# Where the flags that pick the 32nd largest score are computed: one VectorE instruction for two items, or two GpSimd compares

## The chip, the cores and the metric

The kernel runs on one core of a Trainium2 chip. The metric is the device time of one execution in microseconds (us); a run's time is compared as a median over several executions. The engines are TensorE (PE; its weight loads are PEld), VectorE (DVE), ScalarE (ACT), GpSimd (POOL) and SyncE (SP, which here only issues DMAs). Each engine takes its instructions in the order in which the program lists them; between engines, and between dependent instructions of one engine, semaphores make an instruction wait.

## The reference

Attention with top-k selection for 8 batches of 8 heads, 576 queries and keys of 64 dimensions, and then a highway layer over the 512 joined columns:

```python
scores = scale * q @ k.T                       # 576 x 576 for each batch and head
kth = the 32nd largest score of each row
attn = softmax(scores where scores >= kth, else -1e9)
x = attn @ v                                   # heads side by side: 4608 x 512
H = max(x @ w_h, 0);  T = sigmoid(x @ w_t + b_t)
out = T * H + (1 - T) * x
```

What matters here is `kth`: one number for each of the 36864 rows of scores.

## The kernel before

**Units, items and steps.** 128 rows of scores (576 columns) of one head, or two half-filled heads for the rows that are left over, make a unit, called an item here. Two items make a pair. There are 288 items and 144 pairs, and the loop `step(i)` handles pair i in one pass, together with the pairs next to it: scores for pair i+2 on PE, the search for candidates of pair i+1 on DVE, the threshold of pair i, the masking of pair i-1, and the product with V of pair i-3. The last pair is handled in `finish`, the first candidates in `begin`. The order on each engine is written out by hand: the calls in `step` are the program order (`tc.manual_schedule`).

**How the 32nd largest is found.** DVE takes the 8 largest of each sixth of a row (`segments`, L353, 12 instructions a pair). `refine` (L366 to L382) merges these 48 candidates: `high` and `low` are the larger and the smaller of two sorted lists, `neg` is `high` negated, four further 8-largest instructions (L373, L376) and two more (L378, L382) give for each item a lower threshold, `wall[THR]`, about the 24th largest. ACT then counts how many of the 576 scores lie above that threshold (`mask_count`, L397: a sign with an accumulated sum, `csum`), and PE adds a mask to the scores in PSUM (`mask_add`, L410), so that DVE can take the 8 largest below the threshold (`below`, L420). The threshold and these 8 are nine candidates for the 32nd largest. Which of them it is follows from the count: `pidx` holds the nine counts that are possible, and the flags `hit` are one where `csum` equals the entry of `pidx`. The flags are multiplied with the nine candidates (`pick_a`, L436, on POOL) and summed (`pick_b`, L439, on DVE). That sum is `kth`.

**The order around the change in `step(i)`.**

- DVE: 12 of L353 for pair i+1, two L420 for pair i, `high` (L366), `low` (L368), the flags (L426), `neg` (L370), two L373, two L376, `pick_b` (L439), L378, then the masking of pair i-1: L450, L382, L460 (or L465).
- POOL: the biases of the pair (`biases`, L391, which wait for the masking L460 of the step before), a compare of 576 columns with `kth` (`above_one`, L454), one piece of "pool work" of the highway layer (L564, L610, L611 or L624: 512 columns, some 256), the product (`pick_a`, L436), and in most steps the issue of a DMA (L187, L182, L582 or L694).
- ACT: counts, exponentials, copies of scores from PSUM and copies for the highway layer.

In `finish` the flags are made by the same function, and the product with the candidates is DVE's (L996).

Of the kernel before, what the change touches and what calls it, by code (L numbers as in the profile page):

```python
# [10 lines left out]
ALU = mybir.AluOpType  # L11
# [15 lines left out]
def kernel(  # L27
# [10 lines left out]
    nc = tc.nc  # L38
    P = nc.NUM_PARTITIONS
# [54 lines left out]
    NPK = TOP_K - RANK + 1  # L94
    pidx = consts.tile([P, NPK], FP32)
# [15 lines left out]
    csum = consts.tile([P, NU], FP32)  # L111
    nc.vector.memset(wall[:, 0:2, KTH : KTH + 1], 0.0)

    def kth(u):
        return wall[:, u + 2, KTH : KTH + 1]
# [158 lines left out]
    def spare(n):  # L274
        if "t" not in po:
            po.update(t=pso_tile(), n=0)
        for _ in range(n):
            nc.tensor.matmul(  # L278
                po["t"][:, 4 * DE : BANK],
                ident_b[:],  # L280
                cst[:, 0 : BANK - 4 * DE],
                start=True,
                stop=True,
                skip_group_check=True,
            )
# [121 lines left out]
    def mask_add(ps, m1, s):  # L407
        cuts = ((0, MAIN), (MAIN, S)) if s == 0 else ((0, rem), (rem, S))
        for s0, s1 in cuts:
            nc.tensor.matmul(  # L410
                ps[:, s0:s1], ident_b[:], m1[:, s0:s1], start=False, stop=True, skip_group_check=True
            )
# [7 lines left out]
        nc.vector.max(wall[:, u, THR + 1 : KTH], ps)  # L420


    def hits(pair):
        u0, u1 = pair[0], pair[1] + 1
        hit = cpool.tile([P, 2, NPK], FP32, name="hit")
        nc.vector.tensor_tensor(  # L426
            hit[:],
            pidx[:].unsqueeze(1).to_broadcast([P, 2, NPK]),
            csum[:, u0:u1].unsqueeze(2).to_broadcast([P, 2, NPK]),
            ALU.is_equal,  # L430
        )
        return hit

    def pick_a(pair, hit):
# [6 lines left out]
    def above(u, sc):  # L441
        r = epool.tile([P, S], BF16, name="r")
        nc.scalar.activation(r[:], sc, AF.Relu, bias=eb(u), scale=BIGK)  # L443
        return r
# [17 lines left out]
    def keep(u, sc, e):  # L462
        ep = eps_sb[u % NEP]
        pad = (u % 2) * (SP - S)
        return ep, nc.vector.scalar_tensor_tensor(  # L465
            out=ep[:, pad : pad + S],
            in0=sc,
            scalar=kth(u),
            in1=e[:],
            op0=ALU.is_ge,  # L470
            op1=ALU.mult,
        )
# [6 lines left out]
    def transposes(ep):  # L479
        et = etpool.tile([P, nck, P], BF16, name="et")  # L480
        nc.sync.dma_start_transpose(et[:], ep[:])
        return et
# [4 lines left out]
    def values(pair, ets, vb, pso, col):  # L487
        for s, u in enumerate(pair):
            b, qt, heads = units[u]
            r0, ql = row_of(pair), rem if qt == nfull else P  # L490
            for gi, h in enumerate(heads):
                for c in range(nck):
                    vc = (c - s) % nck
                    nc.tensor.matmul(  # L494
                        pso[r0 : r0 + ql, col : col + DE],
                        ets[s][:, c, gi * P2 : gi * P2 + ql],
                        vb[:, h, vc, :],
                        start=(c == 0),
                        stop=(c == nck - 1),
                    )  # L500
                col += DE
        return col

    def pso_tile():
        return ops.tile([P, BANK], FP32, tag="po", name="pso")

    def xs_copy(h0, n, pso, xs, r0=0, r1=P):
        nc.scalar.copy(xs[r0:r1, h0 * DE : h0 * DE + n], pso[r0:r1, 0:n])  # L508
# [145 lines left out]
    def blk_xt(k, ps):  # L654
        ng = shape_of(k["qt"])[1]
        k["xT"] = fpool.tile([P, n_g, P], BF16, name="xT")
        for g in range(ng):
            nc.tensor.transpose(ps[:, g * P : (g + 1) * P], k["x"][:, g * P : (g + 1) * P], ident_f[:])
        nc.scalar.copy(k["xT"][:, 0:ng, :], ps[:, 0 : ng * P].rearrange("p (g j) -> p g j", j=P))
# [32 lines left out]
    def do_add(i):  # L692
        dst, src, then = adds.pop(0)
        nc.gpsimd.dma_start(dst, src, accum_op=ALU.add)  # L694
        stores.append((i + 2, then))
# [247 lines left out]
    def finish():  # L943
        i = NG - 1
        pr, pu = pairs[i], pairs[i - 1]
        cur, old = st[i], st[i - 1]

        def values_of(g, n):
            return values(pairs[g], st[g]["et"], vbs[(B - 1) % 2], po["t"], n)

        def xs_of(qt, h0, n):
            if (B - 1, qt) not in xs_t:
                xs_t[B - 1, qt] = xpool.tile([P, H * DE], FP32, name="xs")
            xs_copy(h0, n, po["t"], xs_t[B - 1, qt])
            po["t"] = pso_tile()
            return dict(b=B - 1, qt=qt, xs=xs_t[B - 1, qt])

        def masked(unit, s, of):
            return keep(unit[s], of["sc"][s], of["e"][s])

        def bank(tile, k):
            return tile[:, k * BANK : (k + 1) * BANK]


        z = blocks[-1]
        values_of(i - 3, 0)
        mask_add(cur["ps"][0], cur["m"][0], 0)
        spare(6)
        while late:
            late.pop(0)()  # L970
        if "xT" not in z:
            blk_xt(z, fps.tile([P, 512], FP32, tag="fp", name="fp"))
        while adds:
            do_add(i)
        relu = above(pu[0], old["sc"][0])
        zh = fps.tile([P, 512], FP32, tag="fp", name="fp")
        ep, last = masked(pu, 1, old)
        old["et"][1] = transposes(ep)
        if pool_work:
            after(do_work(nc.gpsimd, dm), last)  # L980
        below(pr[0], cur["ps"][0])
        mask_add(cur["ps"][1], cur["m"][1], 1)
        project(zh, z["qt"], z["xT"], wh, False)
        below(pr[1], cur["ps"][1])
        es = [expo(u, cur["sc"][s]) for s, u in enumerate(pr)]
        cur["e"] = es
        x1 = xps.tile([P, 3 * BANK], FP32, tag="x", name="xs")
        project(bank(x1, 1), z["qt"], z["xT"], wt, True)
        blk_gate(z, bank(x1, 1))
        n = values_of(i - 2, 2 * DE)  # L990
        ya = xs_of(nfull - 1, H // 2, n)

        hit = hits(pr)
        ep, _ = keep_min(pu[0], old["e"][0], relu)
        old["et"][0] = transposes(ep)
        nc.vector.tensor_tensor(hit[:], hit[:], wall[:, pr[0] : pr[1] + 1, THR:KTH], ALU.mult)  # L996
        pick_b(pr, hit)
        x2 = xps.tile([P, 3 * BANK], FP32, tag="x", name="xs")
        cur["et"] = [etpool.tile([P, nck, P], BF16, name="et") for s in range(2)]
        turned = None  # L1000
        for s, home in enumerate((bank(x2, 1), bank(x1, 0))):
            ep, last = masked(pr, s, cur)
            turned = home.bitcast(BF16)[:, 0:SP]
            for c in range(nck):
                nc.tensor.transpose(turned[:, c * P : (c + 1) * P], ep[:, c * P : (c + 1) * P], ident_b[:])
            nc.scalar.copy(cur["et"][s][:].rearrange("p c q -> p (c q)"), turned)
        sure(0, wall[:, 2 : NU + 2, KTH], 1.0)
        sure(1, wall[:, 0:NU, TOP], -1.0)
        values_of(i - 1, 0)
        blk_norm(ya)  # L1010
        blk_xt(ya, bank(x1, 2))
        n = values_of(i, 0)
        yb = xs_of(nfull, 0, n)
        project(bank(x1, 0), ya["qt"], ya["xT"], wh, False)
        do_work(nc.vector, NG * dm)
        nc.vector.scalar_tensor_tensor(cond[:], wall[:, 0:NU, THR + 1], ABOVE, wall[:, 0:NU, THR], ALU.mult, ALU.add)
        while stores:
            stores.pop(0)[1]()
        sure(2, cond[:], 1.0)
        blk_norm(yb)  # L1020
        blk_xt(yb, bank(x2, 2))
        project(bank(x1, 1), ya["qt"], ya["xT"], wt, True)
        blk_gate(ya, bank(x1, 1))
        blk_diff(z, zh)
        store(*blk_out(z))
        project(bank(x2, 0), yb["qt"], yb["xT"], wh, False)
        bg = fps.tile([P, 512], FP32, tag="fp", name="fp")
        project(bg, yb["qt"], yb["xT"], wt, True)
        for j in range(3):
            nc.tensor.matmul(po["t"][0:1, 0:1], cnt[:, j : j + 1], ones[:], start=(j == 0), stop=(j == 2))  # L1030
        blk_diff(ya, bank(x1, 0))
        store(*blk_out(ya))
        blk_gate(yb, bg)
        nc.vector.tensor_scalar(flag[:], po["t"][0:1, 0:1], 3.0 * P * NU - 0.5, None, ALU.is_ge)
        blk_diff(yb, bank(x2, 0))
        return blk_out(yb)
# [102 lines left out]
```

## Time and profile before

| | |
|---|---|
| median of 3 runs | 806.49 us (806.15 to 808.53) |
| the profiled execution | 806.17 us |
| its span, first to last instruction | 804.5 us |
| granted TensorE clock | 0.996 |
| VectorE busy | 772.8 us, 96% of the span |
| ScalarE busy | 757.2 us, 94% |
| TensorE matmuls busy | 686.7 us, 85% |
| GpSimd busy | 559.9 us, 70% |

"Busy" is the time in which at least one of an engine's instructions is under way. A row of a group ends with the busy time of the group, the mean of one instruction in ns, and behind the bar the idle time of the engine just before these instructions and what ended it. A row of a timeline gives start, duration, engine, line, operation, what is written and read, the count, and in brackets idle time with what ended it. Instructions of one engine overlap: the next one starts while the last one still writes.

### The profile page before, as it was taken

What the parts mean: (1) busy time and instruction counts of PE and PEld (TensorE: products, weight loads), DVE (VectorE), ACT (ScalarE), POOL (GpSimd) and SP (SyncE); (2) the same over time, 40 slices, a digit from 0 to 9 for tenths busy, and PEclk for the clock granted to TensorE, in tenths of its full rate; (3) what the DMA queues carried; (4) which work ended last, traced back from release to release, by engine and by line L of the source; (5) the groups of instructions that cost most, each with busy time, mean ns of one, the idle gap of its engine ahead of it and who ended that gap; (6) DMA issues with size and microseconds to landing.
All of it is one profiled execution on the core that took longest, in us unless ns stands there. A gap on an engine that the chain in (4) does not pass through costs nothing.

```text
span 804.5 us, 20583 instructions
## 1 busy us (share of the span) xinstructions
PE 686.7 (85%) x6369; PEld 494.7 (61%) x6459; DVE 772.8 (96%) x4020; ACT 757.2 (94%) x1401; POOL 559.9 (70%) x712
## 2 busy tenths in 40 slices
PE   7889998888888888888987889888888888988884
PEld 5666766566666666566665666666666566665662
DVE  5999999999999999999999999999999999999996
ACT  5999999999999999999999999999999999999984
POOL 2666867777777767777767776777776777766750
PEclk9999999999999999999999999999999999999998
DMA  6789968996799667998669766898767996555653
GB/s 121 87 137 159 134 116 140 141 143 93 140 152 148 108 96 137 154 131 125 102 135 159 125 113 107 150 156 126 112 121 136 160 124 109 90 106 110 108 90 88
DMA packets 346359, 100.37 MB, mean 125 GB/s; under 512 B 330624, under 2 KB 338432, under 8 KB 346240
## 3 DMA queue, kind: packets, MB, share of 16 engines
q1 hardware_dynamic: 291024, 79.16, 54.1%
q0 software_dynamic: 53536, 19.34, 22.6%
q8 instruction: 53, 0.87, 0.4%
q10 hardware_dynamic: 1680, 0.46, 0.3%
q14 instruction: 66, 0.54, 0.2%
HBM read 31.72 MB, written 9.44 MB: 51 GB/s over the span
## 4 chain that ended last, share of the span: by engine, by line
ACT 37%; DVE 32%; PE 23%; DMA 4%; issue 3%; SPq 1%; another core or an unknown queue 0%; DVEq 0%; ACTq 0%
ACT m L397 15%; DVE wall L420 12%; DVE cand L353 9%; ACT e L416 7%; ACT sc L348 6%; PE pso L278 5%; ACT r L443 4%; PE xs L309 4%; PE xs L326 3%; DVE ep L450 3%; DMA xT<-xb 3%; PE fp L522 3%; PE xs L410 3%; PE pso L494 2%; ACT xs L508 2%
## 5 line engine op out<-in xcount | busy, mean ns | idle before, releaser
L353 DVE MAX8 cand<-xs 128x8 f32<-128x96 f32 x1728 | 297.5, 248 | 11.4 <-PE xs L335 6.2
L278 PE MATMUL pso<-cst,ident_b 128*128 128x252 bf16 x1841 | 246.8, 272 | 42.8 <-ACT xs L508 40.4
L454 POOL TENSOR_SCALAR ro<-sc,wall 128x576 bf16<-128x576 f32 x135 | 232.8, 1724 | 0.0
L416 ACT ACTIVATE e<-sc,be 128x576 bf16<-128x576 f32 x288 | 226.5, 787 | 0.1
L278 PEld LDWEIGHTS <-ident_b 128*128 128x128 bf16 x1841 | 173.4, 98 | 81.4 <-issue 49.5
L420 DVE MAX8 wall<-xs 128x8 f32<-128x576 f32 x288 | 204.3, 751 | 5.6 <-PE xs L410 3.5
L309 PE MATMUL xs<-kT,qT 64*128 64x256 f32 x1024 | 145.3, 400 | 30.6 <-DVE high L366 26.2
L348 ACT COPY sc<-xs 128x1152 f32<-128x1152 f32 x144 | 161.0, 1118 | 0.7 <-DVE cand L353 0.6
L309 PEld LDWEIGHTS xs<-kT,qT 64*128 64x128 f32 x1024 | 93.0, 186 | 61.3 <-issue 37.6
L397 ACT ACTIVATE m<-xs,wall 128x576 int8<-128x576 f32 x144 | 107.4, 746 | 18.2 <-DVE wall L382 17.1
L436 POOL TENSOR_TENSOR hit<-hit,wall 128x18 f32<-128x18 f32 x143 | 32.4, 227 | 121.2 <-DVE hit L426 114.0
L397 ACT ACTIVATE m<-sc,wall 128x576 int8<-128x576 f32 x144 | 111.4, 773 | 0.0
L443 ACT ACTIVATE r<-sc,be 128x576 bf16<-128x576 f32 x143 | 109.9, 769 | 0.0
L410 PE MATMUL xs<-m,ident_b 128*128 128x512 bf16 (+1 forms) x512 | 92.7, 274 | 17.3 <-ACT m L397 15.2
L494 PEld LDWEIGHTS <-et 128*128 128x128 bf16 (+1 forms) x1600 | 68.6, 100 | 19.2 <-issue 3.5
L391 POOL TENSOR_TENSOR be<-wall,fac 128x4 f32<-128x4 f32 x144 | 29.2, 203 | 72.5 <-DVE ep L460 53.7
L410 PEld LDWEIGHTS <-ident_b 128*128 128x128 bf16 x576 | 51.7, 97 | 44.8 <-issue 24.1
L494 PE MATMUL pso<-vb,et 128*128 128x65 bf16 (+1 forms) x1600 | 74.4, 194 | 4.2 <-DMA et<-ep 0.3
L450 DVE TENSOR_TENSOR ep<-e,r 128x576 bf16<-128x576 bf16 x143 | 64.6, 452 | 0.2 <-ACT r L443 0.2
L318 PEld LDWEIGHTS xs<-kd,qT 128*128 128x128 f32 x256 | 38.1, 188 | 42.5 <-issue 42.1
L318 PE MATMUL xs<-kd,qT 128*128 128x128 f32 x256 | 62.5, 326 | 0.0
L460 DVE TENSOR_TENSOR ep<-e,ro 128x576 bf16<-128x576 bf16 x135 | 60.7, 449 | 0.0
(127 smaller groups left out, 1028.9 us busy)
## 6 DMA issues: line engine op xcount, KB each, us to landing
kin<-in_k_dram SPq DMA_DIRECT2D x64, 128.0 KB, 2.9
qin<-in_q_dram SPq DMA_DIRECT2D x62, 128.0 KB, 3.1
out_dram<-s SPq DMA_DIRECT2D x30, 256.0 KB, 2.8
s<-h POOLq DMA_DIRECT2D x29, 256.0 KB, 4.0
et<-ep SPq DMA_TRANSPOSE x286, 3.3
xb<-x POOLq DMA_DIRECT2D x30, 128.0 KB, 3.0
vb<-in_v_dram POOLq DMA_DIRECT2D x28, 128.0 KB, 4.8
vb<-in_v_dram POOLq DMA_DIRECT2D x24, 64.0 KB, 3.1
```

Of the source, the lines that this page charges most:

```text
L278: nc.tensor.matmul(po["t"][:, 4 * DE : BANK], ident_b[:], cst[:, 0 : BANK - 4 * DE], start=True, stop=True, skip_group_check=True,)
L309: nc.tensor.matmul(ps[:, mo + n0 : mo + n0 + 256], qT[r : r + D, hp, qs : qs + P], kT[r : r + D, hp, n0 : n0 + 256], start=(n0 == 0), stop ...
L318: nc.tensor.matmul(ends, qT[:, hp, qs : qs + P], kd[:, hp, :], start=True, stop=True)
L348: nc.scalar.copy(sc[:], both)
L353: nc.vector.max(cand[:, s, :], sc[:, s * SEG : (s + 1) * SEG])
L397: nc.scalar.activation(m1[:].bitcast(I8)[:, 1 : 2 * S : 2], ps, AF.Sign, bias=wall[:, u, THR : THR + 1], scale=ABOVE, accum_out=csum[:, u ...
L410: nc.tensor.matmul(ps[:, s0:s1], ident_b[:], m1[:, s0:s1], start=False, stop=True, skip_group_check=True)
L416: nc.scalar.activation(e[:], sc, AF.Exp, bias=tb(u), scale=scale)
L420: nc.vector.max(wall[:, u, THR + 1 : KTH], ps)
L443: nc.scalar.activation(r[:], sc, AF.Relu, bias=eb(u), scale=BIGK)
L454: nc.gpsimd.tensor_scalar(r[:], sc, kth(u), None, ALU.is_ge)
L494: nc.tensor.matmul(pso[r0 : r0 + ql, col : col + DE], ets[s][:, c, gi * P2 : gi * P2 + ql], vb[:, h, vc, :], start=(c == 0), stop=(c == nc ...
```

## The change

The flags are no longer made by one DVE instruction for both items, which reads `pidx` and `csum` as two broadcast tensors (18 columns), but by two compares on GpSimd, one for each item: nine columns of `pidx` against one number per row, that item's column of `csum`. The product that follows stays on GpSimd, now directly behind the two compares. In the last step (`finish`) the flags stay on VectorE, as two compares. All other instructions keep their places: DVE has 143 instructions less, and on POOL the two compares stand right ahead of the product in each of 143 steps. (`in1=e` for `in1=e[:]` names the same tile.)

```diff
-    def hits(pair):
+    def hits(pair, eng=nc.gpsimd):
         u0, u1 = pair[0], pair[1] + 1
         hit = cpool.tile([P, 2, NPK], FP32, name="hit")
-        nc.vector.tensor_tensor(
-            hit[:],
-            pidx[:].unsqueeze(1).to_broadcast([P, 2, NPK]),
-            csum[:, u0:u1].unsqueeze(2).to_broadcast([P, 2, NPK]),
-            ALU.is_equal,
-        )
+        for s in range(2):
+            eng.tensor_scalar(hit[:, s, :], pidx[:], csum[:, u0 + s : u0 + s + 1], None, ALU.is_equal)
         return hit
...
-            in1=e[:],
+            in1=e,
...
-        hit = hits(pr)
+        hit = hits(pr, nc.vector)
```

## The prediction

> **What bounds the kernel now.** I read the page's first lines, then the busy time of the stretch in which all steps of the loop lie (17.5 to 785 us), then the groups, then one step in order of time. The profiled execution took 806.17 us, of which 804.5 are the span, so 1.67 us lie around it; the median of the three runs is 806.49 us. The sum is made against 806.17.
>
> ```profile
> span 804.5 us, 20583 instructions
> PE 686.7 (85%) x6369; PEld 494.7 (61%) x6459; DVE 772.8 (96%) x4020; ACT 757.2 (94%) x1401; POOL 559.9 (70%) x712
> ACT 37%; DVE 32%; PE 23%; DMA 4%; issue 3%; SPq 1%; another core or an unknown queue 0%; DVEq 0%; ACTq 0%
> core 0: us, PE busy (x) PEld busy (x) DVE busy (x) ACT busy (x) POOL busy (x), PEclk, DMA share, GB/s
> 17.50:785.00 767.50, 665.16 (x6182) 479.98 (x6270) 751.28 (x3923) 740.42 (x1369) 557.33 (x699) 1.00 0.79 126
> ```
>
> In the loop DVE is busy for 751.28 of 767.50 us: 16.2 us idle over 143 steps. ACT has 27.1 us idle. Both bind, in turns. GpSimd (POOL) has 210 us idle, so by totals the move looks free. But what counts is the moment at which GpSimd works, and that shows only in one step in order of time (DVE and POOL rows, and one of ACT).
>
> ```profile
> 261.26 0.19 ACT L397 ACTIVATION_READ_ACCUMULATOR m<-sc,wall 128x1 f32 x1
> 262.10 1.41 DVE L420 MAX8 wall<-xs 128x8 f32<-128x576 f32 x2
> 262.16 1.26 POOL L624 TENSOR_TENSOR h<-h,tt 128x512 f32<-128x512 f32 x1
> 263.43 0.19 DVE L366 TENSOR_TENSOR high<-cand 128x48 f32<-128x48 f32 x1
> 263.53 0.20 DVE L368 TENSOR_TENSOR low<-cand 128x48 f32<-128x48 f32 x1
> 263.65 0.17 DVE L426 TENSOR_TENSOR hit<-pidx,csum 128x18 f32<-128x18 f32 x1
> 263.74 0.18 DVE L370 TENSOR_SCALAR neg<-high 128x48 f32<-128x48 f32 x1
> 263.83 0.26 DVE L373 MAX8 en<-low 128x8 f32<-128x24 f32 x2
> 263.90 0.23 POOL L436 TENSOR_TENSOR hit<-hit,wall 128x18 f32<-128x18 f32 x1 [0.48 <-DVE hit L426]
> 264.18 0.15 DVE L439 TENSOR_REDUCE wall<-hit 128x2 f32<-128x18 f32 x1
> ```
>
> See here: POOL ends its pool work at 263.42, sits idle for 0.48 us, and starts the product (L436) 0.08 us after the flags (L426) end on DVE. In just that idle stretch DVE runs `high`, `low` and the flags, each of which reads two tensors of SBUF. The product starts 0.47 us after `high`.
>
> **What is removed.** 143 instructions L426 of 0.17 us. They overlap their neighbours, so one takes from its start to that of `neg`: 263.74 - 263.65 = 0.09 us. Not all of that comes back. `neg` reads `high` and the first L373 reads `low`, so the flags now fill time in which these are still being written. The trace has one refinement without flags, ahead of the loop:
>
> ```profile
> 12.49 0.21 DVE L366 TENSOR_TENSOR high<-cand 128x48 f32<-128x48 f32 x1
> 12.62 0.20 DVE L368 TENSOR_TENSOR low<-cand 128x48 f32<-128x48 f32 x1
> 12.73 0.18 DVE L370 TENSOR_SCALAR neg<-high 128x48 f32<-128x48 f32 x1
> 12.85 0.27 DVE L373 MAX8 en<-low 128x8 f32<-128x24 f32 x2
> ```
>
> From `high` to L373 it is 0.36 us there and 0.40 with flags; from `low`, 0.23 against 0.30. I take 0.05 us a step: 143 x 0.05 = 7.2 us off DVE (bounds: 143 x 0.04 = 5.7 and 143 x 0.09 = 12.9). In the last step the flags stay on DVE as two compares; the second is hidden by the wait for ReLU that follows there, and I cost it at nothing (0.1 us without that cover).
>
> **What is added.** Two compares of 9 columns a step on POOL, ahead of the product. The trace has no such small compare there. Nearest rows:
>
> ```profile
> L454 POOL TENSOR_SCALAR ro<-sc,wall 128x576 bf16<-128x576 f32 x135 | 232.8, 1724 | 0.0
> L436 POOL TENSOR_TENSOR hit<-hit,wall 128x18 f32<-128x18 f32 x143 | 32.4, 227 | 121.2 <-DVE hit L426 114.0 <-DVE neg L370 6.5 <-DMA et<-ep 0.7
> L391 POOL TENSOR_TENSOR be<-wall,fac 128x4 f32<-128x4 f32 x144 | 29.2, 203 | 72.5 <-DVE ep L460 53.7 <-DVE wall L382 10.8 <-DVE ep L465 5.3
> ```
>
> One compare lies between 0.20 (4 columns) and 1.72 us (same operation, 576 columns). I take 0.22, by the 18- and 4-column rows; two started 0.03 us into one another (as L454 starts behind L391) hold POOL for about 0.41 us. They wait for ACT's counts, which were there at 261.45, two microseconds before POOL was free: this wait costs nothing. Queued behind them on POOL are the product, one DMA issue, and the biases (L391). The product now waits for the second compare and for L420, no longer for the flags; with POOL free early it could start at about 263.59 instead of 263.90.
>
> **What is moved onto the path: a hold on DVE.** In a few steps of before, POOL was still busy when `high` came up:
>
> ```profile
> L366 DVE TENSOR_TENSOR high<-cand x144: 183/190/655, 12.5 to 780.3; 128x48 f32<-128x48 f32 x144
> 283.76 1.27 POOL L610 TENSOR_TENSOR s<-h,x 128x512 f32<-128x512 f32 x1 [0.81 <-ACT h L609]
> 284.44 0.66 DVE L366 TENSOR_TENSOR high<-cand 128x48 f32<-128x48 f32 x1
> 285.01 0.20 DVE L368 TENSOR_TENSOR low<-cand 128x48 f32<-128x48 f32 x1
> ```
>
> `high` has a median of 0.19 us, but here it lasted 0.66, until POOL's sum was done (285.03), and `low` started 0.57 us after it where 0.10 is usual: DVE lost 0.47 of the 0.59 us that POOL still had. So a hold costs the rest of POOL's work less 0.12 us. The compares fill just the gap that kept this rare. `high` comes up 0.47 us before the product's present start, so it is held in each step where POOL's idle time before the product is below 0.47 + 0.41 - 0.12 = 0.76 us. These are 75 of 143 rows; the first and the last:
>
> ```profile
> 81.61 0.23 POOL L436 TENSOR_TENSOR hit<-hit,wall 128x18 f32<-128x18 f32 x1 [0.36 <-DVE hit L426]
> 769.16 0.23 POOL L436 TENSOR_TENSOR hit<-hit,wall 128x18 f32<-128x18 f32 x1 [0.50 <-DVE hit L426]
> ```
>
> Their mean idle time is 0.54 us, so `high` comes 0.22 us later in each: 75 x 0.22 = 16.5 us. If POOL lets DVE in between the two compares, the second compare and the product come late for L439 instead, which has only 0.05 us in hand (263.90 + 0.23 against 264.18); I cost both cases alike.
>
> By the Trainium skill ("SBUF — State Buffer", section "Who interferes with whom"), a VectorE instruction with two SBUF inputs and a GpSimd one that reads SBUF exclude each other for the whole instruction, and the later one blocks fully. By that rule the 0.12 us fall away; 90 rows would count instead of 75, and the hold would come to 26.5 us in place of 16.5. The trace's 0.47 of 0.59 us speaks for a little less, and I keep it.
>
> **The product's new place.** `neg` has one input; whether POOL holds that kind too shows in another tensor-scalar of DVE:
>
> ```profile
> L557 DVE TENSOR_SCALAR rinv<-xs x38: 157/162/483, 50.2 to 770.1; 128x8 f32<-128x8 f32 x31, 128x4 f32<-128x4 f32 x7
> 147.04 0.99 POOL L187 DMA_DIRECT2D vb<-in_v_dram  x1 [0.29 <-issue]
> 147.51 0.48 DVE L557 TENSOR_SCALAR rinv<-xs 128x8 f32<-128x8 f32 x1
> ```
>
> It lasted 0.48 instead of 0.16 us, to the end of POOL's issue. So the product, when it starts up to 0.31 us earlier, can run beside `neg` (due at about 263.67, product until 263.82) and hold it by 0.15 us, or 0.03 after the 0.12 are taken off. I take 0.05 us a step: 143 x 0.05 = 7.2 us (bounds 0 and 143 x 0.15 = 21).
>
> **The sum.** DVE's stream: -7.2 + 16.5 + 7.2 = +16.5 us. How much of it reaches the end? The chain of work that ended last has 50 pieces of L426 among 143 steps, first and last
>
> ```profile
> 28.44 0.09 DVE hit L426
> 763.86 0.09 DVE hit L426
> ```
>
> so a small change on DVE counts for 35%; in the other steps ACT or PE binds. A longer DVE binds in more steps, at most in all. I take 0.6: 0.6 x 16.5 = 9.9 us, and 806.17 + 9.9 = **816 us**, 1.2% over the median.
>
> **The rivals.**
> A, *the change does what it is for* (faster): the hold is small, because POOL gives way between the compares or the pair takes 0.22 us. With 0.22 for 0.41 the bound is 0.57, and 42 rows lie under it, 4.7 us in all. With `neg` untouched that gives -7.2 + 4.7 = -2.5 us, or -12.9 + 4.7 = -8.2 with the whole pitch saved. At 35%: 805.3 or 803.3; the latter is its price, and it decides from a pair of about 0.3 us down. Against it: nothing on POOL in this trace takes less than 0.19 us.
> B, *the delay is absorbed*: DVE has 16.2 us idle in the loop, and +16.5 fits into it nearly exactly. Then no change: 806. Against it: much of that idle time lies in waits for PE, whose work itself waits for DVE.
> C, *the compares are dear*: 0.40 us each, 0.77 the pair. The bound becomes 1.12, 112 rows lie under it by 0.45 on average, 50.5 us; with 0.6 of it, 806.17 + 0.6 x 50.5 = 836 us. For it: POOL's only compare is slow, 1.72 us at 576 columns where a two-input 512-column sum takes 1.27.
>
> **How the numbers follow.** The forecast (slower, 809 to 827) has a chance of 0.55, A 0.14, B and small losses up to 809 0.18, C 0.13. About 0.3% (2.4 us) is what a measurement can tell from no change. Faster than 804.1: 0.13, most of A. Within 804.1 to 808.9: 0.19. Slower: 0.68. The range takes in A and the forecast with compares of 0.3 us (pair 0.57, bound 0.92, about 30 us of hold; 806.17 + 0.6 x (30 + 7.2 - 7.2) = 824) and full pass-through of the taken sum (823), and leaves out C's end: 803 to 829.
>
> **What would show it.** Right: the group of `high` (L366) rises from a mean of 0.20 us to about 0.31, its maximum stays near POOL's longest operation, and DVE's busy time in the loop does not fall although 143 instructions are gone; idle time before the product falls well under 114 us; compares show about 0.2 us. Wrong: `high` stays at 0.19 to 0.20 us (then A), compares of 0.3 us or more (then towards C), L439 waiting for the product although `high` was on time (the loss is then a late product, not a hold), or DVE idle time falling by the whole sum (B).

## The result, and the profile after

The changed kernel takes 816.08 us (median of 4 runs, 815.47 to 817.4) against 807.51 us of the kernel before on the same chip (806.15 to 809.87): a ratio of 1.0105 with a 95% interval of 1.0075 to 1.0135, 8.6 us slower. The profiled execution took 815.8 us with a span of 814.1.

The first lines of the page, and the busy time of the loop (17.5 to 795 us now), of the changed kernel:

```profile
span 814.1 us, 20896 instructions
PE 697.6 (86%) x6459; PEld 494.6 (61%) x6459; DVE 773.7 (95%) x3878; ACT 758.8 (93%) x1401; POOL 649.9 (80%) x998
DVE 35%; ACT 22%; PE 17%; POOL 17%; issue 4%; DMA 4%; SPq 1%; POOLq 0%; DVEq 0%; ACTq 0%
17.50:795.00 777.50, 675.78 (x6271) 479.94 (x6272) 752.24 (x3781) 742.28 (x1369) 646.59 (x983) 1.00 0.79 124
```

DVE has 142 instructions fewer (143 less in the steps, one more in `finish`) and is busy for as long as before. POOL was not on the chain of work that ended last and has 17% of it now. The lines that changed, by operation and in the order of a step (of each: minimum, median and maximum in ns):

```profile
L427 POOL TENSOR_SCALAR hit<-pidx,csum x286: 302/310/629, 14.6 to 788.7; 128x9 f32<-128x9 f32 x143
L366 DVE TENSOR_TENSOR high<-cand x144: 178/190/654, 12.3 to 790.0; 128x48 f32<-128x48 f32 x144
L370 DVE TENSOR_SCALAR neg<-high x144: 172/179/189, 12.6 to 790.2; 128x48 f32<-128x48 f32 x144
```

A compare of nine columns takes 0.31 us, not 0.22. `neg` is never held (at most 0.189 us). `high` keeps its median. Its mean, in the group rows, rises by 0.02 us:

```profile
L427 POOL TENSOR_SCALAR hit<-pidx,csum 128x9 f32<-128x9 f32 x286 | 89.7, 326 | 1.1 <-ACT m L397 1.1
L432 POOL TENSOR_TENSOR hit<-hit,wall 128x18 f32<-128x18 f32 x143 | 34.6, 242 | 32.8 <-DVE high L366 24.5 <-DVE neg L370 0.5
L366 DVE TENSOR_TENSOR high<-cand 128x48 f32<-128x48 f32 x144 | 32.0, 222 | 0.0
L435 DVE TENSOR_REDUCE wall<-hit 128x2 f32<-128x18 f32 x144 | 23.3, 162 | 7.1 <-POOL hit L432 5.0
```

POOL's idle time before the product (L432) fell from 121.2 to 32.8 us. In 54 steps POOL was early, and the product still waits for L420 (in 53 of them it starts 0.15 us after the end of L420; the row names `high`, the next instruction). In the other 89 it starts 0.08 us after its own compares. And the sum (L435) waits for the product; no such row stood in the waits of before. One step of the changed kernel in order of time:

```profile
265.37 1.41 DVE L420 MAX8 wall<-xs 128x8 f32<-128x576 f32 x2
265.44 1.26 POOL L620 TENSOR_TENSOR h<-h,tt 128x512 f32<-128x512 f32 x1
266.68 0.64 POOL L427 TENSOR_SCALAR hit<-pidx,csum 128x9 f32<-128x9 f32 x2
266.70 0.30 DVE L366 TENSOR_TENSOR high<-cand 128x48 f32<-128x48 f32 x1
266.93 0.20 DVE L368 TENSOR_TENSOR low<-cand 128x48 f32<-128x48 f32 x1
267.04 0.18 DVE L370 TENSOR_SCALAR neg<-high 128x48 f32<-128x48 f32 x1
267.15 0.27 DVE L373 MAX8 en<-low 128x8 f32<-128x24 f32 x2
267.34 0.25 DVE L376 MAX8 en<-neg 128x8 f32<-128x24 f32 x2
267.40 0.23 POOL L432 TENSOR_TENSOR hit<-hit,wall 128x18 f32<-128x18 f32 x1
267.66 0.17 DVE L435 TENSOR_REDUCE wall<-hit 128x2 f32<-128x18 f32 x1
```

Two things are to be seen. `high` lasts 0.30 us, to 267.00, when the first compare (266.68 + 0.31) is done: the hold, 0.12 us here. Then POOL goes on with the second compare to 267.32, waits 0.08 us for its own result, multiplies to 267.63, and the sum starts at 267.66: 0.32 us after the two L376 began, where it is 0.17 without a wait. The waits row counts only 5.0 us for that. The rest is not idle time, because the second L376 is still under way while the sum waits; it shows only in the distance from start to start.

So I added up, for all of DVE's instructions from 17.5 us on, the time from the start of each to the start of the next, by group (us; the five columns on the right are experiments told below). The last row is then nothing but the time from 17.5 us to DVE's last instruction in the profiled execution.

| | before | changed | swap | its control | extra compares | extra memsets | no flags |
|---|---|---|---|---|---|---|---|
| flags | 12.9 | 0.3 | 0.3 | 12.8 | 12.8 | 12.7 | 0.3 |
| `high` and `low` (hold) | 33.9 | 40.7 | 40.8 | 33.7 | 42.8 | 33.7 | 33.6 |
| `neg` and L373 | 39.2 | 42.6 | 42.8 | 38.9 | 39.2 | 39.5 | 43.6 |
| L376, to the next instruction | 24.4 | 35.9 | 24.6 | 24.0 | 28.2 | 24.3 | 24.2 |
| L378, to the next instruction | 13.3 | 13.8 | 16.0 | 12.1 | 13.0 | 13.3 | 14.1 |
| all of DVE | 780.4 | 789.9 | 781.7 | 778.6 | 788.4 | 782.0 | 778.9 |

Before to changed: -12.6 for the flags, of which `neg` and L373 take back 3.4, presumably because they now wait for what `high` and `low` write; +6.8 for the hold; +11.5 for the sum that waits for the product. That is +9.1 of the +9.5 us of DVE's stream.

### The profile page after: what moved, and what is told of

Same layout as the page of the kernel before. It is cut to its first block, busy times and chain, and to the rows that moved or that the text cites. A ratio compares the mean times of both kernels' runs of the same rounds, so it can differ in the third digit from the quotient of the medians.

```text
span 814.1 us, 20896 instructions
## 1 busy us (share of the span) xinstructions
PE 697.6 (86%) x6459; PEld 494.6 (61%) x6459; DVE 773.7 (95%) x3878; ACT 758.8 (93%) x1401; POOL 649.9 (80%) x998
## 4 chain that ended last, share of the span: by engine, by line
DVE 35%; ACT 22%; PE 17%; POOL 17%; issue 4%; DMA 4%; SPq 1%; POOLq 0%; DVEq 0%; ACTq 0%
DVE wall L420 12%; ACT m L397 11%; DVE cand L353 9%; POOL ro L450 6%; DVE ep L446 4%; ACT e L416 4%; PE xs L326 3%; ACT sc L348 3%; PE xs L410 3%; PE pso L278 3%; DMA xT<-xb 3%; PE fp L518 2%; POOL hit L427 2%; ACT r L439 2%; POOL h L607 2%
## 5 line engine op out<-in xcount | busy, mean ns | idle before, releaser
L420 DVE MAX8 wall<-xs 128x8 f32<-128x576 f32 x288 | 203.8, 747 | 7.5 <-PE xs L410 5.2
L397 ACT ACTIVATE m<-xs,wall 128x576 int8<-128x576 f32 x144 | 107.3, 745 | 25.6 <-DVE wall L382 23.5
L410 PE MATMUL xs<-m,ident_b 128*128 128x512 bf16 (+1 forms) x576 | 107.0, 285 | 21.9 <-ACT m L397 19.9
L427 POOL TENSOR_SCALAR hit<-pidx,csum 128x9 f32<-128x9 f32 x286 | 89.7, 326 | 1.1 <-ACT m L397 1.1
L446 DVE TENSOR_TENSOR ep<-e,r 128x576 bf16<-128x576 bf16 x143 | 64.5, 451 | 0.7 <-issue 0.7
L432 POOL TENSOR_TENSOR hit<-hit,wall 128x18 f32<-128x18 f32 x143 | 34.6, 242 | 32.8 <-DVE high L366 24.5
```

What stands on the lines that cost most here:

```text
L397: nc.scalar.activation(m1[:].bitcast(I8)[:, 1 : 2 * S : 2], ps, AF.Sign, bias=wall[:, u, THR : THR + 1], scale=ABOVE, accum_out=csum[:, u ...
L410: nc.tensor.matmul(ps[:, s0:s1], ident_b[:], m1[:, s0:s1], start=False, stop=True, skip_group_check=True)
L427: eng.tensor_scalar(hit[:, s, :], pidx[:], csum[:, u0 + s : u0 + s + 1], None, ALU.is_equal)
```

## The experiments

Two theories. **Theory 1, late product:** POOL's time ahead of the product is now longer than DVE's way to the sum. **Theory 2, hold:** the compares keep `high` and `low` waiting, as the forecast had it. All runs are compared with runs of the kernel before on the same chip, 807.46 us in the first four, 806.95 us in the last four.

**The sum later, and its control.**

```diff
-        if live:
-            pick_b(pr, hit)
         next(ra, None)
         masked(0)
+        if live:
+            pick_b(pr, hit)
```

> The changed kernel, with the sum of the flagged candidates (pick_b) issued on DVE behind the first masking instead of ahead of L378, some 0.45 us later in DVE's order. Theory 1 (late product: from the start of `high` to L378 a step of the changed kernel is 57 ns longer than before, of which +81 ns are the sum waiting for POOL's product, +26 ns the hold of `high`, and -47 ns the missing flags): the 81 ns go, 143 x 0.08 = 11.5 us of DVE's stream, so 803 to 807 us, not slower than before. Theory 2 (hold: `high` kept waiting by the compares is what costs, as the forecast had it): `high` is held as much as in the changed kernel, so the time stays at 812 us or more.

> The control: the kernel before with the same later place of the sum. There the product is in time, so both theories expect no change, within 1.5 us of the kernel before.

Measured: 815.96 us, ratio 1.0106 (1.0091 to 1.0122); the control, in which nothing was late, 810.37 us, 1.0038 (1.0024 to 1.0051). Taken alone, the time lies in theory 2's range and 9 us above theory 1's. But the control missed as well: the new place costs by itself 2.9 us. Ahead of L378 the sum had filled the time in which L378 waits for the second L376; without it that time stands empty (the idle time before L378 is 4.9 us in both runs, 0 before). Against its control the changed kernel is 5.6 us slower here, not 8.6, although no sum waits for its product any more (each product ends at least 0.23 us ahead of its sum). By this pair the late product is worth 3.0 us. The figure is rough: the four runs lie at 813.31 and at 815.93 to 816.28 us. And a move that costs something itself separates the theories badly; hence the exchange further down.

**Two extra compares, two extra memsets**, on POOL ahead of the product, to a tile that nobody reads; the flags stay on DVE.

```diff
             hit = hits(pr)
+            for s in range(2):
+                nc.gpsimd.tensor_scalar(spill[:, s, 0:NPK], pidx[:], csum[:, pr[s] : pr[s] + 1], None, ALU.is_equal)
...
+                nc.gpsimd.memset(spill[:, s, 0:224], 0.0)
             pick_a(pr, hit)
```

> The kernel before (flags on DVE, as they were) plus two compares a step on POOL ahead of the product, of the changed kernel's form, written to a tile that nobody reads. Theory 1: POOL's 0.64 us ahead of the product make it late as in the changed kernel, and DVE has the flags as well: 815 to 824 us. Theory 2 expects the same time, by the hold of `high`; the pair with the next run tells them apart. Should the compares only cost through what waits for their result, it stays at 806 to 808 us.

> As the run with extra compares, but with two memsets of 224 columns in their place, which should take about 0.3 us each and read nothing from SBUF. Theory 1 (POOL's time counts, whatever it does): within 3 us of the run with extra compares, `high` not held. Theory 2 (reading SBUF beside `high` counts): within 2 us of the kernel before.

Measured: with compares 813.6 us, ratio 1.0077 (1.0064 to 1.0091), 1.4 us under the range; with memsets 807.64 us, 1.0002 (0.9993 to 1.0011), nothing. One step with compares:

```profile
264.98 0.60 POOL L857 TENSOR_SCALAR spill<-pidx,csum 128x9 f32<-128x9 f32 x2
264.99 0.31 DVE L367 TENSOR_TENSOR high<-cand 128x48 f32<-128x48 f32 x1
265.22 0.37 DVE L369 TENSOR_TENSOR low<-cand 128x48 f32<-128x48 f32 x1
```

and one with memsets:

```profile
263.76 0.50 POOL L857 MEMSET spill<- 128x224 f32 x2
263.81 0.18 DVE L367 TENSOR_TENSOR high<-cand 128x48 f32<-128x48 f32 x1
263.92 0.20 DVE L369 TENSOR_TENSOR low<-cand 128x48 f32<-128x48 f32 x1
```

Both pairs start at the moment of `high` and occupy POOL for half a microsecond or more. Beside the compares, `high` and `low` take 0.31 and 0.37 us; beside the memsets, which read nothing, 0.18 and 0.20. In the table the hold is 8.9 us with compares and none with memsets. What holds `high` and `low` is that POOL reads SBUF, not that it is busy. The Trainium skill ("SBUF — State Buffer", section "Who interferes with whom") says just this: a VectorE instruction with two SBUF inputs contends with a GpSimd instruction that reads SBUF, not with one that only writes it. Here the trace agrees (0.31 and 0.37 against 0.18 and 0.20 us). The compares also made the product late at times (L376: +3.8 us), less than in the changed kernel, where the product also waits for their result and DVE has no flags to run in the meantime. The memsets were not quite without effect. They held `neg`, which has one input, in 14 of 144 steps (0.22 to 0.30 us; the row gives minimum, median and maximum in ns):

```profile
L371 DVE TENSOR_SCALAR neg<-high x144: 172/178/298, 12.3 to 782.2; 128x48 f32<-128x48 f32 x144
```

The time did not show it.

**The exchange, and its control.**

```diff
-        for _ in range(5):
+        for _ in range(4):
             next(ra, None)
-        if live:
-            pick_b(pr, hit)
         next(ra, None)
         masked(0)
+        next(ra, None)
+        if live:
+            pick_b(pr, hit)
```

> The changed kernel, but on DVE the first masking (L446) changes places with the sum: L376, L446, L378, sum, L382. The sum comes about 0.5 us later and so cannot wait for the product, and each place between dependent instructions of the refinement keeps one instruction that fills it, which the run with the sum behind both did not do (its control lost 3 us). Theory 1 (the late product costs 11.5 of the +9.5 us of DVE's stream, the hold 6.8, the missing flags give back about 9.5): 804 to 807 us, at or under the kernel before. Theory 2 (the hold alone): 812 us or more.

> The control: the kernel before with the same exchange of the first masking and the sum. Both theories expect no change, within 1.5 us; if the exchange itself costs something, the run before is to be read against this one.

Measured: 808.44 us, ratio 1.0022 (1.0012 to 1.0032); the control 805.29 us, 0.9978 (0.9969 to 0.9987). The changed kernel's loss is gone but for 1.5 us against the kernel before. The time is 1.4 us over theory 1's range and 3.6 under theory 2's. The control came 1.7 us under the kernel before, where 1.5 was the most expected. A step of the changed kernel with the sum in its new place:

```profile
258.54 0.67 POOL L427 TENSOR_SCALAR hit<-pidx,csum 128x9 f32<-128x9 f32 x2
258.91 0.20 DVE L366 TENSOR_TENSOR high<-cand 128x48 f32<-128x48 f32 x1
259.29 0.22 POOL L432 TENSOR_TENSOR hit<-hit,wall 128x18 f32<-128x18 f32 x1
259.45 0.25 DVE L376 MAX8 en<-neg 128x8 f32<-128x24 f32 x2
259.62 0.44 DVE L446 TENSOR_TENSOR ep<-e,r 128x576 bf16<-128x576 bf16 x1
259.98 0.18 DVE L378 SCALAR_TENSOR_TENSOR cand<-en 128x16 f32<-128x16 f32 x1
260.06 0.17 DVE L435 TENSOR_REDUCE wall<-hit 128x2 f32<-128x18 f32 x1
```

The product is ready at 259.51 and the sum asks for it at 260.06: here nothing waits. L376 costs 24.6 us instead of 35.9, and the hold is what it was (40.8). But in 33 of 143 steps the sum is late after all, as in this one:

```profile
156.78 0.69 POOL L427 TENSOR_SCALAR hit<-pidx,csum 128x9 f32<-128x9 f32 x2
157.47 0.44 DVE L446 TENSOR_TENSOR ep<-e,r 128x576 bf16<-128x576 bf16 x1
157.56 0.44 POOL L432 TENSOR_TENSOR hit<-hit,wall 128x18 f32<-128x18 f32 x1
157.83 0.21 DVE L378 SCALAR_TENSOR_TENSOR cand<-en 128x16 f32<-128x16 f32 x1
158.03 0.17 DVE L435 TENSOR_REDUCE wall<-hit 128x2 f32<-128x18 f32 x1
```

The product runs beside the masking (L446), which reads two tensors of SBUF, and lasts 0.44 us, where 0.23 is usual in the changed kernel; in all 33 steps it ends 0.08 to 0.09 us after the masking, and the sum starts 0.03 us later. So the hold also works the other way: DVE keeps POOL waiting. These waits stand in the row of L378, 16.0 us against 12.1 in the control.

Against its control, where only the engine of the flags differs, the rest is 808.44 - 805.29 = 3.2 us: the hold and the late sums that are left, less what the missing flags bring. So by this pair at least 5.4 of the 8.6 us are the late product, against 3.0 by the pair with the sum behind both. Both theories hold in part; the late product is shown, its exact share is not. The control itself is the fastest kernel that does all the work: 0.2% faster than the one before.

**No flags.**

```diff
-        nc.vector.tensor_tensor(hit[:], pidx..., csum..., ALU.is_equal)
...
-        nc.gpsimd.tensor_tensor(hit[:], hit[:], wall[:, u0:u1, THR:KTH], ALU.mult)
+        nc.gpsimd.tensor_tensor(hit[:], fixed[:], wall[:, u0:u1, THR:KTH], ALU.mult)
```

> The kernel before without the flags in the 143 steps: the product takes a fixed row of flags made once, so the fifth candidate is taken whatever the count says (the comparison with the counts is left out). POOL does nothing more than before, so this is the gain that the change could have had. The forecast's step expects 0.05 us a step off DVE, 7.2 us, of which 35 to 100% reach the end: 800 to 805 us. A rival, that ACT binds as soon as DVE is shorter, expects 806 us or more.

Measured: 803.95 us, ratio 0.9965 (0.9951 to 0.9978), 3.0 us saved. In DVE's stream the flags go (-12.6), `neg` and L373 take back 4.4, `high` and `low` give 0.3: -8.5 us, 0.06 a step, of which 35% arrive. This was all that the change could gain. It also bounds the hold: 3.0 saved and 3.2 lost in the exchange pair make 6.2 us, and the extra compares, with the flags in place, cost 6.1. Both sums contain late sums too (3.9 and 3.8 us of DVE's stream beside 7.1 and 8.9 of hold), so 6 us is an upper bound; divided by these shares of the stream, the hold is worth some 4 us, an estimate.

**Two compares on DVE.**

```diff
-            hit = hits(pr)
+            hit = hits(pr, nc.vector)
```

> The changed kernel with its two compares a step on DVE, as in its last step, and POOL as before. It separates the form from the engine: one more instruction a step on DVE, 0.09 to 0.13 us each, 13 to 19 us of DVE's stream of which 0.5 to 1 arrives: 813 to 825 us by all theories; if the form were nearly free on DVE, 807 to 809.

Measured: 823.78 us, ratio 1.0216 (1.02 to 1.0232), 16.8 us slower. From start to start one of these compares takes 38.4 / 286 = 0.134 us, against 0.09 for the one instruction with both items: 25.5 us more of DVE's stream. The form has its price on either engine.

## Why the prediction came out, point by point

The forecast was 816 us, and 816.08 were measured. The mechanism was half right, and the agreement to 0.1 us is luck: the forecast added 9.9 us to 806.17, and 8.6 us were measured on 807.51. Of the two costs that the sum had, one came out at less than half and the other did not come at all, a third that it had not counted apart made up for much of them, and a share of 0.6 was taken where nearly 1 was right.

- **The flags' worth, 7.2 us of DVE's stream, 35% of a small saving arriving: right.** Without flags 8.5 us went, and 3.0 of it arrived. The refinement ahead of the loop, the one without flags, had shown that their place was half empty.
- **One compare at 0.22 us: too low.** It takes 0.31 (302/310/629 ns), 0.60 the pair and more where DVE holds it (0.64 in the step above), where 0.41 was taken, and the product waits another 0.08 us for the compares' result, which the forecast left out.
- **The hold of `high`, 16.5 us in 75 steps: the mechanism right, the size not.** `high` and `low` together lost 6.8 us, and `high` exceeds 0.2 us in 50 steps (9 before). The step that failed is the one that took the pair for one block of 0.41 us: `high` waits for the end of the compare under way, not for the pair (266.99 to 267.00 in the step above). The second compare then holds `low` in some steps: `low` took 0.22 us or more in 29 steps, up to 0.375, where before none took more than 0.205. The longest `high`, 0.654, still stands behind POOL's 512-column sum, as before. By experiment the hold costs at most some 6 us of time.
- **"If POOL lets DVE in between ... I cost both cases alike": this case it was.** The text had the late product only as the other form of the same cost. It is a cost of its own: the sum started late in 57 of 143 steps (over 0.095 us behind the start of the second L376, where 0.085 is usual), 11.5 us of DVE's stream, between 3.0 and something over 5.4 us of the time by the two pairs. The prediction had named a sum that waits although `high` is on time as a sign of being wrong; in 36 of these 57 steps `high` took less than 0.22 us. Another such sign, compares of 0.3 us or more, came too.
- **The hold of `neg`, 7.2 us: wrong.** None of the 144 `neg` was longer than 0.189 us: the product ran beside it in 67 steps and a compare in 75, and neither held it. The row from which the forecast took this term shows another pair, `rinv` beside the issue of a DMA.
- **The sum +16.5 of DVE's stream and the share of 0.6: both off, their product near (9.9 us forecast, 8.6 measured).** The groups of the refinement that changed grew by 9.1 us together, and all other groups of DVE by 0.4: hardly anything was taken up elsewhere, so nearly all of it arrived. That a delay in the middle of the refinement puts off ACT's counts (idle time before them 17.1 us before, 23.5 now) fits this, but was not tried apart.
- **The rivals.** A would have needed a pair under 0.3 us, and found 0.60 or more (its 4.7 us of hold come out of the rows as 4.6, and four memsets of 0.10 us at the start are shorter than its 0.19; neither changes its price). B was refuted: the time grew, and DVE's idle time in the loop rose from 16.2 to 25.3 us instead of falling. C's price of a compare (0.40) lay as far above the measured 0.31 us as the forecast's below, but a hold for the whole pair did not come. The two waits of DVE and ACT in the changed kernel (us in total, times, longest):

```profile
ACT m L397 <- DVE wall L382: 23.5, 59, 0.9
DVE wall L435 <- POOL hit L432: 5.0, 22, 0.3
```

What stays open: why the exchange of masking and sum alone makes the kernel before 1.7 us faster was not tried apart, and what the late product costs in time is known only roughly. Of DVE's stream the trace gives more: 56 of the 57 late steps have a compare of more than 0.33 us (0.31 is usual), and only 2 of the other 86 do. That DVE held these compares, as it held the product in the exchange, is likely but was not tried by itself. Counted step by step with all else left as it is, the late sums lost 11.8 us; without what the compares took over 0.31 us it would be 7.5, without the wait of 0.08 us 7.2, without both 3.9. This is an estimate from one trace; no run took these parts away one by one.

## What to carry to other kernels

Work moved to an engine with idle time is free only if it also falls into that idle time: look at what the other engine does in just that stretch, and at how long after it the result is asked for. Where two instructions keep each other waiting, count both delays. An instruction between two dependent ones may cost less than its length, and so bring less when it goes. And look for a wait in the distance from start to start: where a neighbour is still under way, the idle column hides most of it (5.0 of 11.5 us here).

## What the runs showed of the hardware that was not expected

- On POOL a compare with one number per row takes 0.31 us for 9 columns and 1.73 for 576: a line through these two sizes (which differ in the type that is written) gives 0.29 us and 2.5 ns a column. The two-input product of 18 columns takes 0.23.
- A POOL instruction that reads SBUF and a two-input one of DVE hold each other: beside a compare `high` took 0.31 us (0.19 alone), and beside the masking the product took 0.44 (0.23 alone). Memsets on POOL left `high` and `low` at 0.18 and 0.20 us, but held the one-input `neg` in 14 steps (up to 0.298 us), which the compares never did (at most 0.189).
- On DVE two compares of 9 columns with one number per row (0.134 us each from start to start) cost three times one two-input compare of 18 (0.09).
